# One fused attention and MLP kernel: where lam multiplies the channel mix, and how the planner orders the engine queues

## The chip, the cores and the metric

The kernel runs on one core of a Trainium2 chip. The metric is the device time of one execution in microseconds (us): 377.52 is the median of 8 runs of the kernel before, from 376.94 to 379.87. TensorE (PE) multiplies matrices into PSUM, which has eight banks; VectorE (DVE), ScalarE (ACT) and GpSimd (POOL) work on elements; SyncE (SP) issues nearly all DMA transfers. Every engine works through its own queue in order.

## What is computed

Batch 8, 8 heads of 64, sequence 576, model width 512. Inputs and output are float32.

```
kv  = einsum('bhsd,bhde', k, v)          # linear attention, no softmax
o   = einsum('bhsd,bhde', q, kv)
x   = o / sqrt(mean(o*o over the head) + 1e-6) * g_norm      # heads side by side: (b, s, 512)
a1  = alpha1 * x + beta1
u   = x + lam * (w_tok @ a1)             # token mix, 576 x 576
a2  = alpha2 * u + beta2
out = u + lam * (max(a2 @ w_ch1, 0) @ w_ch2)                 # channel mix, 512 -> 2048 -> 512
```

## The kernel before

The program is not written in the order in which it runs. `Prog.op` records each operation with a cost for each engine that could do it, the tiles that it reads and writes, and a priority. `Prog.schedule` is a list scheduler that plays the whole program through with these costs. It picks the engine, the PSUM bank and the place in the queue of each operation, and `emit` writes the queues out in that order. On the chip each queue is then fixed: an instruction whose input is late holds up all that stand behind it on its engine. A load is believed to land at `dma_free + 2.0`, where `dma_free` starts at 1.2 us and grows by the operation's `dma_us`: 2.8 for a megabyte, 1.4 for half of one, 0.9 for a tail of 64 rows.

A batch goes through these steps, and the scheduler interleaves them over neighbouring batches:

- `load` and `round_in`: q, k and v come in blocks of 1 MB into six staging buffers `st` and are cast to float32r (L521, L414, L415); rows 512 to 575 come apart as tails (L529). Casts go to ScalarE or VectorE, whichever the planner finds free.
- `kv` (L594) and `qtr` (L583, with `identr`): 128x128 float32r matmuls. They are kind "F", which the planner likes to alternate with the bf16 matmuls of another step.
- `norm`: o by L583, its square on ScalarE (L651), the sum over a head (L653), root (L656), reciprocal (L659) and the product (L664) on VectorE and ScalarE. From it come `rt`, the input of the token mix, on VectorE (L666), and x itself on GpSimd (L669).
- `tok` (L887): five matmuls for each of five row chunks; VectorE adds the result to x (L895), and a cast gives `ub`.
- `ut` (L915): transposes of `ub`, evicted as `a2t` with alpha2 and beta2 (L924, L926).
- `ch1` (L957): 64 matmuls of 512 columns for an even batch, 128 of 320 for an odd one, which takes the tail rows of two batches along. Relu into `ht` on ScalarE or VectorE (L942, L943).
- `ch2` (L977): 16 matmuls for each row chunk, four chunks for an even batch and five for an odd one. VectorE adds the result to x in place (L985), and SP stores x. For batch 0 the order runs over blocks of w_ch2 and then chunks, so its four chunks end close together. lam is already in the weights: `load_w2` multiplies each block of w_ch2 by `lam_bc` as it casts it to bf16, one half on VectorE and one on GpSimd (L1166).

Batch 0 has a path of its own in `first`, in two halves of four heads each. Its squares' sums are made by matmuls with a wide selector `sel` onto 4 rows (L781), the root is taken there (L788), five small transposes bring it into columns (L792), and VectorE takes the reciprocal (L795). The token weights are cast with row sums (L1109, L1110), transposed (L1134) and copied from PSUM. While nothing of `ch1` has begun, `dummy` puts matmuls on ones (L1060) where PE would be idle, in any PSUM bank if three are free. Weights come in this order after batch 0: w_tok, four blocks of w_ch1 (cast by ScalarE, L414), batch 1, four blocks of w_ch2.

Of the kernel before, what the change touches and what calls it, by code (L numbers as in the profile page):

```python
# [7 lines left out]
F32 = mybir.dt.float32  # L8
# [6 lines left out]
NB = 8  # L15
# [8 lines left out]
class Op:  # L24
    __slots__ = ("cost", "fn", "deps", "raw", "alloc", "tiles", "pri", "idx", "eng", "kind",
                 "start", "end", "pos", "waits", "inc", "lat", "clock", "sem", "succ", "left",
                 "ready", "keep", "soft", "tag")

    def __init__(self, cost, fn, pri, idx):
        self.cost, self.fn, self.pri, self.idx = cost, fn, pri, idx  # L30
        self.deps, self.raw = set(), set()
        self.alloc, self.tiles = [], []
        self.start = self.end = self.pos = self.eng = None
        self.waits, self.inc, self.lat, self.clock, self.sem = [], False, None, None, None
        self.succ, self.left, self.ready, self.kind, self.keep, self.soft = [], 0, 0.0, None, 0, set()

# [13 lines left out]
class Prog:  # L50
# [20 lines left out]
    def op(self, engs, fn, r=(), w=(), pri=0.0, dma_us=None, kind=None, keep=0, after=()):  # L71

        o = Op(dict(engs), fn, pri, len(self.ops))
        o.lat, o.kind, o.keep, o.tag = dma_us, kind, keep, self.tag
        self.ops.append(o)
# [44 lines left out]
    def schedule(self):  # L120
# [11 lines left out]
        dma_free = 1.2  # L132
# [4 lines left out]
        last_kind = None  # L137
        seq = []
# [27 lines left out]
        def bank_ok(b):  # L166
            tile = owner[b]
            return tile is None or all(x.end is not None and x.end <= t + 1e-9 for x in tile.ops)
# [28 lines left out]
        def finish(e, o):  # L197
            return max(free[e], t) + o.cost[e]

        def choose(e):  # L200
            q = ready[e]
            back, pick, second = [], None, None
            while q:
# [12 lines left out]
                if not fits(o):  # L216
                    continue
# [16 lines left out]
        while left:  # L234
            progressed = True
            while progressed:
                progressed = False
                for e in engines:
# [19 lines left out]
                    free[e] = t + cost  # L258
                    if o.lat is not None:
# [21 lines left out]
            if self.warm is not None and free["PE"] <= t + 1e-9 and t > 0.5:  # L281
                o = self.dummy(t, owner, bank_ok, since)
# [22 lines left out]
    def dummy(self, t, owner, bank_ok, since):  # L305
        okb = [b for b in range(8) if bank_ok(b)]
        if len(okb) < 3:
            return None
        b = min(okb, key=since)
        tile = PTile(self, 1)  # L310
        tile.bank = b
        o = Op({"PE": 0.22}, lambda e, n, tile=tile: self.warm_fn(e, tile), 0, 10 ** 6 + len(self.ops))
        self.ops.append(o)
        o.idx = len(self.ops) + 10 ** 6
# [3 lines left out]
        if any(y.end is None or y.end > t for y in self.warm_deps):  # L318
            self.ops.pop()
            return None  # L320
        if owner[b] is not None:
            o.deps.update(owner[b].ops)
        tile.ops.append(o)
        owner[b] = tile
# [83 lines left out]
def pool_us(n, two=True):  # L408
    return 0.2 + n * (2.5 if two else 1.05) / 1000.0
# [8 lines left out]
def bass_transnormer_attn__then__resmlp_affine_kernel(  # L418
# [15 lines left out]
    with ExitStack() as stack:  # L434
# [9 lines left out]
        vcol = sb("vcol", [8, 128], F32)  # L444
        cols = sb("cols", [128, 8], F32)
        ones = sb("ones", [1, 128], F32)
# [4 lines left out]
        sel = sb("sel", [128, 2, 128], F32R)  # L451
# [17 lines left out]
        yn = sb("yn", [128, 3, DM], F32)  # L469
        xm = sb("xm", [128, 2, 4, DM], F32)  # L470
# [17 lines left out]
        rs4 = w2f[0:4, 0:2 * TP].rearrange("p (x s) -> p x s", x=2)  # L488
        e1 = w2f[:, 1280:1792]
        sel0 = w2f[:, 1792:2048].rearrange("p (i c) -> p i c", i=2)  # L490
# [24 lines left out]
        def load_main(n, src, b, eng, pri, halves=None):  # L515
# [3 lines left out]
            for x in halves or (None,):  # L519
# [4 lines left out]
                    w=STK(i) if x is None else [("st", i, x)], dma_us=2.8 if x is None else 1.4,  # L524
                    pri=pri, kind="L")

        def load_tail(n, tile, src, b, lo, eng, pri):
# [3 lines left out]
                w=[key], dma_us=0.9, pri=pri, kind="L")  # L531

        def load(b, pri):
            P.tag = "load.%d" % b
            if b == 0:
# [5 lines left out]
                load_tail("q", qft, q, b, 0, "SP", pri)  # L541
                load_main("k", k, b, "SP", pri, (1,))
                load_main("v", v, b, "SP", pri, (1,))
                load_main("q", q, b, "SP", pri, (1,))
# [11 lines left out]
        def round_in(b, pri):  # L556
            P.tag = "round_in.%d" % b
            for n, dst in (("q", qr), ("k", kr), ("v", vr)):
                i = held[n, b]
                pieces = [(c, c + 2, 0, 8) for c in (0, 2)]  # L560
                for c0, c1, h0, h1 in pieces:
                    def f(e, m, i=i, c0=c0, c1=c1, h0=h0, h1=h1, n=n, d=dst):
# [7 lines left out]
                         w=[(n + "r", x, y) for x in range(c0, c1) for y in hs], pri=pri)  # L570
            for n, lo, dst in (("k", 0, krt), ("v", 64, vrt)):
                P.op({"DVE": 0.45, "ACT": 0.65}, lambda e, m, lo=lo, d=dst: copy_to(
                    e, m, flat(d[0:64]), flat(kvft[lo:lo + 64])), r=[n + "ft"], w=[n + "rt"], pri=pri)
            if b % 2 == 0 or b == 1:
                rows = {0: slice(0, 64), 1: slice(64, 128)}.get(b, slice(0, 128))
                P.op({"DVE": 0.45, "ACT": 0.65}, lambda e, m: copy_to(
                    e, m, flat(qrt[rows]), flat(qft[rows])), r=["qft0", "qft1"][:b + 1], w=["qrt"], pri=pri)
# [8 lines left out]
        def kv(b, pri):  # L586
            P.tag = "kv.%d" % b
            t = P.ptile(1)
            for pr in range(4):
                for c in range(5):  # L590
                    def f(e, _, pr=pr, c=c):
                        a = flat(kr[:, c, 2 * pr:2 * pr + 2, :] if c < 4 else krt[:, 2 * pr:2 * pr + 2, :])
                        m = vr[:, 2 * pr:2 * pr + 2, c, :] if c < 4 else vrt[:, 2 * pr:2 * pr + 2, :]
                        return e.matmul(t.flat()[:, 128 * pr:128 * pr + 128], a, m,  # L594
                                        start=(c == 0), stop=(c == 4))
                    P.op(F, f, r=["krt", "vrt"] if c == 4 else [("kr", c, pr // 2), ("vr", c, pr // 2)],
                         w=[t], pri=pri, kind="F", keep=2, after=[("kvc", b % 2, x) for x in range(4)])
            for h in range(2):
                rows = slice(64 * h, 64 * h + 64)
                P.op({"ACT": act_us(256), "DVE": dve_us(256)}, lambda e, m, h=h, rows=rows: copy_to(  # L600
                    e, m, kvc[rows, b % 2, :, 64 * h:64 * h + 64],
                    t.flat(rows).rearrange("p (r x) -> p r x", r=4)[:, :, 64 * h:64 * h + 64]),
                    r=[t], w=[("kvc", b % 2, pr) for pr in range(4)], pri=pri - 5)
# [32 lines left out]
        def norm(b, pri):  # L636
            P.tag = "norm.%d" % b
            def chunk(c):
# [6 lines left out]
                for pr in range(4):  # L645
# [22 lines left out]
                    r=[("yn", s3), "ge1"], w=[rkey(b, c)], pri=p - 2)  # L668
# [7 lines left out]
        def first(pri):  # L676
# [6 lines left out]
            def rounding(x):  # L683
                P.tag = "round.0%d" % x
                for n, dst in (("k", kr), ("v", vr), ("q", qr)):
                    i = held[n, 0]
                    hs = slice(4 * x, 4 * x + 4)
                    for c in (0, 2):
                        def f(e, m, i=i, c=c, n=n, d=dst):
# [5 lines left out]
                             r=[("st", i, x)], w=[(n + "r", y, x) for y in (c, c + 1)], pri=pri)  # L695

            P.tag = "round.t"
            for n, lo, dst in (("k", 0, krt), ("v", 64, vrt)):
                P.op({"DVE": 0.45, "ACT": 0.65}, lambda e, m, lo=lo, d=dst: copy_to(
                    e, m, flat(d[0:64]), flat(kvft[lo:lo + 64])), r=[n + "ft"], w=[n + "rt"], pri=pri)  # L700
            P.op({"DVE": 0.45, "ACT": 0.65}, lambda e, m: copy_to(
                e, m, flat(qrt[0:64]), flat(qft[0:64])), r=["qft0"], w=["qrt"], pri=pri)

            def attend(x):
# [13 lines left out]
                for h in range(2):  # L718
                    rows = slice(64 * h, 64 * h + 64)
                    P.op({"ACT": act_us(128), "DVE": dve_us(128)}, lambda e, m, h=h, rows=rows, t=t: copy_to(  # L720
                        e, m, kvc[rows, 0, 2 * x:2 * x + 2, 64 * h:64 * h + 64],
                        t.flat(rows).rearrange("p (r y) -> p r y", r=2)[:, :, 64 * h:64 * h + 64]),
                        r=[t], w=KVK, pri=pri)
# [4 lines left out]
                    r=["g"] + KVK, w=[("kr", 0, x)], pri=pri + 3)  # L728
# [38 lines left out]
                for i in range(2):  # L767
# [4 lines left out]
                        kind="T", keep=1)  # L772
                P.op({"ACT": act_us(128)}, lambda e, _, t=t: e.activation(
# [3 lines left out]
                ts, tt = P.ptile(1), P.ptile(1)  # L777
                for t, n in ((ts, 512), (tt, 64)):
                    for i in range(2):
                        pr = 2 * x + i  # L780
                        P.op({"PE": 0.216 if n == 512 else 0.117}, lambda e, _, t=t, n=n, i=i, pr=pr: e.matmul(  # L781
                            t.flat()[:, 0:n], sel[:, i, :],
                            sqt[:, pr, :] if n == 512 else sqtt[:, pr, 0:64],
                            start=(i == 0), stop=(i == 1)),
                            r=["sel", (("vr", 0, x) if i == 0 else ("vr2", x)) if n == 512 else ("kr", 1, x)],
                            w=[t, ("sums", x)], pri=pri + 3, kind="T")
                for t, lo, n in ((ts, 0, 512), (tt, 512, 64)):
                    P.op({"ACT": act_us(n)}, lambda e, _, t=t, lo=lo, n=n: e.activation(  # L788
                        rs4[:, x, lo:lo + n], t.flat(slice(0, 4))[:, 0:n], ACT.Sqrt, bias=eps[0:4, :],
                        scale=1.0 / DH), r=["eps", t, ("rs4", 2)], w=[("rs4", x, lo)], pri=pri)  # L790
                for c in range(5):
                    P.op({"PE": 0.1}, lambda e, _, c=c: e.transpose(  # L792
                        tt.flat()[:, 128 + 4 * c:132 + 4 * c], rs4[:, x, 128 * c:128 * c + 128],
# [464 lines left out]
```

## Time and profile before

| What | Measured |
|---|---|
| median of 8 runs | 377.52 us |
| the profiled execution | 378.22 us |
| its span, first to last instruction | 376.4 us |
| PE busy | 362.8 us, 96% of the span |
| DVE busy | 225.9 us, 60% |
| ACT busy | 176.7 us, 47% |
| POOL busy | 86.6 us, 23% |
| granted TensorE clock, mean over the span | 0.993 |
| read from HBM, written | 38.20 MB, 9.44 MB |
| PE matmul groups L957, L977, L887 | 146.8, 140.1, 50.6 us |

In the profile, times count from the first instruction. A row names the engine, the source line of the kernel, the operation, and what is written from what; `x8` after it is a count of instructions. In brackets stands how long the engine was idle before it, and what let it go on. "PEld" is the weight load that belongs to a matmul and overlaps the matmul before it. Matmul ends are modelled, so neighbouring matmuls overlap in the rows, and their pace is read from start to start.

### The profile page before, as it was taken

What the parts mean: (1) busy time and instruction counts of PE and PEld (TensorE: products, weight loads), DVE (VectorE), ACT (ScalarE), POOL (GpSimd) and SP (SyncE); (2) the same over time, 40 slices, a digit from 0 to 9 for tenths busy, and PEclk for the clock granted to TensorE, in tenths of its full rate; (3) what the DMA queues carried; (4) which work ended last, traced back from release to release, by engine and by line L of the source; (5) the groups of instructions that cost most, each with busy time, mean ns of one, the idle gap of its engine ahead of it and who ended that gap; (6) DMA issues with size and microseconds to landing.
All of it is one profiled execution on the core that took longest, in us unless ns stands there. A gap on an engine that the chain in (4) does not pass through costs nothing.

```text
span 376.4 us, 5601 instructions
## 1 busy us (share of the span) xinstructions
PE 362.8 (96%) x2258; PEld 224.4 (60%) x2258; DVE 225.9 (60%) x390; ACT 176.7 (47%) x310; POOL 86.6 (23%) x73
## 2 busy tenths in 40 slices
PE   8998699999999999999999999999999999999994
PEld 2786465569775564556865565557755544557641
DVE  5578569995985688539936595539534682520011
ACT  2689646666864256125741266134731274116400
POOL 4641087610441133003500123003500340000000
PEclk9999989999999999999999999999999999999999
DMA  6999999999959228311000120011000210020021
GB/s 197 312 340 361 274 383 310 286 279 319 306 141 311 91 58 290 73 57 56 2 2 22 62 57 0 2 56 57 0 2 28 84 29 1 30 84 2 0 84 56
DMA packets 47797, 47.99 MB, mean 128 GB/s; under 512 B 14096, under 2 KB 38680, under 8 KB 47772
## 3 DMA queue, kind: packets, MB, share of 16 engines
q1 hardware_dynamic: 47520, 47.47, 42.3%
q8 instruction: 17, 0.28, 0.3%
q10 hardware_dynamic: 252, 0.18, 0.2%
q14 instruction: 8, 0.07, 0.1%
HBM read 38.20 MB, written 9.44 MB: 127 GB/s over the span
## 4 chain that ended last, share of the span: by engine, by line
PE 76%; DMA 9%; DVE 6%; SPq 4%; ACT 2%; issue 1%; DVEq 0%; ACTq 0%
PE ps L977 32%; PE ps L957 27%; PE ps L887 10%; DMA st<-in_moe_w_ch_dram 4%; DMA st<-in_v_dram 3%; PE ps L583 3%; DMA kvft<-in_v_dram 2%; PE ps L915 2%; PE ps L594 2%; SPq L521 2%; SPq L529 2%; DVE w L1166 1%; ACT w L414 1%; DVE ht L943 1%; DVE small L653 1%; SPq L1017 1%
## 5 line engine op out<-in xcount | busy, mean ns | idle before, releaser
L957 PE MATMUL ps<-a2t,w 128*128 128x320 bf16 (+1 forms) x768 | 146.8, 332 | 2.1 <-ACT kvc L414 0.7
L977 PE MATMUL ps<-w,ht 128*128 128x512 bf16 x576 | 140.1, 381 | 0.1
L957 PEld LDWEIGHTS ps<-a2t,w 128*128 128x128 bf16 x768 | 73.4, 98 | 44.7 <-DVE ht L943 1.5
L942 ACT ACTIVATE ht<-ps 128x640 bf16<-128x640 f32 (+1 forms) x105 | 68.0, 649 | 47.1 <-PE ps L957 46.7
L977 PEld LDWEIGHTS ps<-w,ht 128*128 128x128 bf16 x576 | 54.5, 98 | 59.1 <-DVE yn L664 0.6
L669 POOL TENSOR_TENSOR xm<-yn,g_bc 128x512 f32<-128x512 f32 x28 | 46.0, 1642 | 167.7 <-DVE yn L664 167.2
L985 DVE TENSOR_TENSOR xm<-ps,xm 128x512 f32<-128x512 f32 x32 | 21.9, 688 | 55.5 <-PE ps L977 55.0
L651 ACT ACTIVATE sq<-ps 128x512 f32<-128x512 f32 (+1 forms) x35 | 20.6, 590 | 49.0 <-PE ps L583 48.9
L895 DVE TENSOR_TENSOR xm<-ps,xm 128x512 f32<-128x512 f32 x28 | 19.3, 690 | 38.0 <-PE ps L887 36.8
L887 PE MATMUL ps<-rt,wt 128*128 128x512 bf16 x140 | 37.3, 381 | 0.0
L594 PE MATMUL ps<-vr,kr 128*128 128x128 f32 x112 | 34.6, 394 | 2.6 <-DVE ht L943 2.6
L583 PE MATMUL ps<-kvc,qt 128*128 128x128 f32 x112 | 33.2, 386 | 0.5 <-DVE ht L943 0.5
L583 PE MATMUL ps<-identr,qr 128*128 128x128 f32 x112 | 31.2, 374 | 0.9 <-ACT qr L414 0.9
L924 ACT ACTIVATE a2t<-ps,cols 128x640 bf16<-128x640 bf16 (+1 forms) x15 | 11.7, 829 | 41.1 <-PE ps L915 41.1
L653 DVE TENSOR_REDUCE small<-sq 128x8 f32<-128x512 f32 (+1 forms) x35 | 23.6, 675 | 10.3 <-ACT sq L651 10.0
L594 PEld LDWEIGHTS ps<-vr,kr 128*128 128x128 f32 x112 | 23.2, 207 | 3.4 <-DVE ht L943 3.1
L664 DVE TENSOR_TENSOR yn<-ps,small 128x512 f32<-128x512 f32 (+1 forms) x35 | 24.0, 685 | 0.5
L666 DVE TENSOR_TENSOR rt<-yn,ge 128x512 bf16<-128x512 f32 x28 | 24.0, 856 | 0.5
L583 PEld LDWEIGHTS ps<-kvc,qt 128*128 128x128 f32 x112 | 22.3, 200 | 3.0 <-DVE ht L943 0.8
L583 PEld LDWEIGHTS ps<-identr,qr 128*128 128x128 f32 x112 | 22.0, 200 | 1.5 <-DVE a2t L926 1.0
L887 PEld LDWEIGHTS ps<-rt,wt 128*128 128x128 bf16 x140 | 13.5, 98 | 15.2
L414 ACT ACTIVATE qt<-ps 128x512 fp32r<-128x512 f32 (+1 forms) x29 | 15.7, 556 | 7.0 <-PE ps L583 6.7
(145 smaller groups left out, 376.4 us busy)
## 6 DMA issues: line engine op xcount, KB each, us to landing
st<-in_moe_w_ch_dram SPq DMA_DIRECT2D x8, 1024.0 KB, 12.5
out_dram<-xm SPq DMA_DIRECT2D x32, 256.0 KB, 2.3
st<-in_q_dram SPq DMA_DIRECT2D x7, 1024.0 KB, 7.9
st<-in_k_dram SPq DMA_DIRECT2D x7, 1024.0 KB, 10.5
st<-in_v_dram SPq DMA_DIRECT2D x7, 1024.0 KB, 12.3
ht<-in_moe_w_tok_dram SPq DMA_DIRECT2D x2, 576.0 KB, 9.5
kvft<-in_k_dram SPq DMA_DIRECT2D x8, 128.0 KB, 9.2
kvft<-in_v_dram SPq DMA_DIRECT2D x8, 128.0 KB, 7.7
```

The source lines that it names most:

```text
L583: P.op(F, lambda e, _: e.matmul(t.flat()[:, 128 * pr:128 * pr + 128], a(), m(), start=True, stop=True), r=r, w=[t], kind="F", **kw)
L594: return e.matmul(t.flat()[:, 128 * pr:128 * pr + 128], a, m, start=(c == 0), stop=(c == 4))
L651: P.op({"ACT": act_us(512)}, lambda e, _: e.activation(flat(sq[rows, s2]), t.flat(rows), ACT.Square), r=[t], w=[("sq", s2)], pri=p)
L653: P.op({"DVE": dve_us(512)}, lambda e, _: e.tensor_reduce(out=small[rows, s4], in_=sq[rows, s2], axis=AX.X, op=ALU.add), r=[("sq", s2)], w ...
L664: P.op({"DVE": dve_us(512)}, lambda e, _: e.tensor_tensor(out=hview(yn[rows, s3, :]), in0=hview(t.flat(rows)), in1=bc, op=ALU.mult), r=[t, ...
L666: P.op({"DVE": dve_us(512), "POOL": pool_us(512)}, lambda e, _: e.tensor_tensor(out=rto, in0=yn[rows, s3, :], in1=ge1[rows, :], op=ALU.mul ...
L669: P.op({"POOL": pool_us(512)}, lambda e, _: e.tensor_tensor(out=hview(x), in0=hview(yn[rows, s3, :]), in1=g_bc[rows, None, :].to_broadcast ...
L887: return e.matmul(t.flat(), wt[:, sc, col:col + 128], rt[:, sc, :] if sc < 4 else rtt[:], start=(sc == 0), stop=(sc == 4))
L942: return e.activation(dst, src(), ACT.Relu)
L957: return e.matmul(o, w1[:, dj, 128 * fj:128 * fj + 128], m, start=(dj == 0), stop=(dj == 3))
L977: P.op({"PE": 0.216}, lambda e, _: e.matmul(t.flat(), ht[:, fj, 128 * c:128 * c + 128], w2[:, fj, :], start=(fj == 0), stop=(fj == 15)), r ...
L985: P.op({"DVE": dve_us(512)}, lambda e, _: e.tensor_tensor(out=x, in0=t.flat(), in1=x, op=ALU.add), r=[t] + keys, w=keys, pri=p - 2)
```

## The change

Six things change together.

1. lam leaves the weights. `load_w2` only casts, on ScalarE, VectorE or GpSimd. In `ch2` VectorE multiplies the PSUM result by `lam_bc` into a new SBUF tile `lc` (one buffer), and GpSimd adds `lc` to x in place; in the last batch VectorE may do the add.
2. [...] Loads start at 3.4 us and take 3.0 a megabyte, 1.5 a half, 1.0 a tail.
3. The warming matmuls have bank 7 for themselves until `ch1` begins.
4. In `first`, the squares' sums come as ten matmuls straight into columns, so the five transposes go; the two halves of `kvc` are evicted without a wait for each other; the second half of q is loaded ahead of those of k and v; one more product of `rt` goes to GpSimd; the token weights are transposed once all five casts are done, and their copies alternate between ScalarE and VectorE; `ut(0)` puts two groups into one PSUM bank and evicts all four on VectorE.
5. `kv(1)` streams each operand twice (256 columns, two PSUM tiles) and is no longer kind "F".
6. Priorities at the start change; casts of w_ch1 wait, in the plan only, for the last root of batch 0, and those of the fourth block may go to GpSimd in place of VectorE.

```diff
-        dma_free = 1.2
+        dma_free = 3.4
+        ports = [0.0]
+        def shares(e, o):
+            return o.lat is None and (e == "POOL" or e == "DVE" and o.port)
...
         def bank_ok(b):
+            if b == 7 and self.warm is not None:
+                return False
...
         def finish(e, o):
-            return max(free[e], t) + o.cost[e]
+            at = max(free[e], t)
+            if shares(e, o):
+                at = max(at, ports[0])
+            return at + o.cost[e]
...
+                if shares(e, o) and ports[0] > t + 1e-9:
+                    continue
...
+                    if shares(e, o):
+                        ports[0] = t + cost
...
 def pool_us(n, two=True):
-    return 0.2 + n * (2.5 if two else 1.05) / 1000.0
+    return 0.2 + n * (2.2 if two else 0.9) / 1000.0
...
+        lc = sb("lc", [128, DM], F32)
...
                 load_main("q", q, b, "SP", pri, (0,))
                 load_tail("q", qft, q, b, 0, "SP", pri)
+                load_main("q", q, b, "SP", pri, (1,))
                 load_main("k", k, b, "SP", pri, (1,))
                 load_main("v", v, b, "SP", pri, (1,))
-                load_main("q", q, b, "SP", pri, (1,))
...
         def kv(b, pri):
-            t = P.ptile(1)
+            wide = b == 1
+            tiles = [P.ptile(1) for _ in range(2 if wide else 1)]
...
+                        if wide:
+                            o = tiles[pr // 2].flat()[:, 256 * (pr % 2):256 * (pr % 2) + 256]
+                            m = m[:, None].to_broadcast([128, 2, 2, DH])
...
-                ts, tt = P.ptile(1), P.ptile(1)
-                for t, n in ((ts, 512), (tt, 64)):
+                ts = P.ptile(1)
+                for c in range(5):
                     for i in range(2):
                         pr = 2 * x + i
-                        P.op({"PE": 0.216 if n == 512 else 0.117}, lambda e, _, t=t, n=n, i=i, pr=pr: e.matmul(
-                            t.flat()[:, 0:n], sel[:, i, :],
-                            sqt[:, pr, :] if n == 512 else sqtt[:, pr, 0:64],
+                        P.op({"PE": 0.12}, lambda e, _, c=c, i=i, pr=pr: e.matmul(
+                            ts.flat()[:, 4 * c:4 * c + 4],
+                            sqt[:, pr, 128 * c:128 * c + 128] if c < 4 else sqtt[:, pr, :],
+                            sel[:, i, :], start=(i == 0), stop=(i == 1)),
...
+                P.root = P.op({"ACT": 0.25}, lambda e, _, ro=ro: e.activation(
+                    ro, ts.flat()[:, 0:20], ACT.Sqrt, bias=eps[:], scale=1.0 / DH),
+                    r=["eps", ts], w=[("rs", x)], pri=pri)
+                P.op({"DVE": 0.25}, lambda e, _, ro=ro: e.reciprocal(ro, ro), r=[("rs", x)],
+                     w=[("rs", x)], pri=pri)
...
-                    P.op({"POOL": pool_us(256 * n)} if x == 0 else {"DVE": dve_us(256 * n)},
+                    P.op({"POOL": pool_us(256 * n)} if x == 0 or c0 == 0 else {"DVE": dve_us(256 * n)},
...
+                    o = P.op({"ACT": act_us(n, 2), "DVE": 0.53 if n == 512 else dve_us(n)} if b else
+                             {"DVE": 0.53}, g, r=[t, "cols"], w=[("a2t", dj)], pri=pri - 5)
+            for djs in ((0, 1), (2, 3)) if b == 0 else ((0,), (1,), (2,), (3,)):
+                group(djs)
...
-                P.op({"DVE": dve_us(512)}, lambda e, _: e.tensor_tensor(
-                    out=x, in0=t.flat(), in1=x, op=ALU.add), r=[t] + keys, w=keys, pri=p - 2)
+                o = P.op({"DVE": dve_us(512)}, lambda e, _: e.tensor_tensor(
+                    out=lc[:], in0=t.flat(), in1=lam_bc[:], op=ALU.mult), r=[t, "lam"],
+                    w=["lc"], pri=p - 2)
+                o.raw.update(o.deps)
+                P.op({"POOL": pool_us(512)} if b < NB - 1 else {"POOL": pool_us(512), "DVE": dve_us(512)},
+                     lambda e, _: e.tensor_tensor(out=x, in0=x, in1=lc[:], op=ALU.add),
+                     r=["lc"] + keys, w=keys, pri=p - 2, port=True)
...
-                P.op({"ACT": act_us(512)} if qn < 3 else {"ACT": act_us(512), "DVE": dve_us(512, 2)}, f, r=STK(i),
-                     w=[("w1", qn, j)], pri=pri)
+                P.op({"ACT": act_us(512)} if qn < 3 else {"ACT": act_us(512), "POOL": pool_us(512, False)}, f,
+                     r=STK(i), w=[("w1", qn, j)], pri=pri).soft.add(P.root)
...
-                P.op({"POOL": pool_us(1024)} if hh else {"DVE": dve_us(1024)}, lambda e, _, hh=hh: e.tensor_tensor(
-                    out=w2[:, 4 * n + 2 * hh:4 * n + 2 * hh + 2, :],
-                    in0=st[:, i, 1024 * hh:1024 * hh + 1024].rearrange("p (j c) -> p j c", j=2),
-                    in1=lam_bc[:, None, :].to_broadcast([128, 2, DM]), op=ALU.mult),
-                    r=STK(i) + ["lam"], w=[("w2", n, hh)], pri=pri + 70)
+                P.op({"ACT": act_us(1024), "DVE": dve_us(1024, 2), "POOL": pool_us(1024, False)},
+                     lambda e, m, hh=hh: copy_to(
+                    e, m, w2[:, 4 * n + 2 * hh:4 * n + 2 * hh + 2, :].rearrange("p j c -> p (j c)"),
+                    st[:, i, 1024 * hh:1024 * hh + 1024]),
+                    r=STK(i), w=[("w2", n, hh)], pri=pri + 70, port=True)
...
-            if o.pri < -500 and o.tag == "sums.01":
-                o.pri -= 2
+            if o.pri < -500 and o.tag == "wt":
+                o.pri -= 4
+            if o.pri < -500 and o.tag in ("kv.01", "qtr.01", "sums.01"):
+                o.pri -= 6
             if o.pri < -500 and o.tag[:2] == "w1":
-                o.pri += 30
+                o.pri = -480 + 4 * int(o.tag[3])
```

## Prediction

> **What bounds the kernel now.** I read the page's busy rows and slices first, then a table of stretches, then the order of time around the one bad stretch. The slices (40 of 9.4 us each; tenths busy, tenths of the clock, tenths of the DMA engines):
>
> ```profile
> PE   8998699999999999999999999999999999999994
> DVE  5578569995985688539936595539534682520011
> PEclk9999989999999999999999999999999999999999
> DMA  6999999999959228311000120011000210020021
> ```
>
> TensorE is the bound from slice 6 to the end; the only hole is slice 5 (38 to 47 us), and the only dip of the clock follows in slice 6. Until slice 10 the DMA engines are full. So a change that touches VectorE, ScalarE or GpSimd is worth something in three places only: the front (until the first channel product runs without a break, at 38 us), the hole, and the tail after the last matmul. The stretches (us; busy of PE, PEld, DVE, ACT, POOL; clock; DMA):
>
> ```profile
> 26.90:38.00 11.10, 9.61 (x82) 7.21 (x81) 9.99 (x26) 10.19 (x19) 1.72 (x4) 1.00 1.07 364
> ...
> 43.00:46.00 3.00, 0.44 (x2) 0.19 (x1) 2.31 (x4) 1.85 (x3) 0.00 (x0) 1.00 1.10 261
> 46.00:51.00 5.00, 4.65 (x23) 3.08 (x22) 2.93 (x4) 2.47 (x5) 2.30 (x1) 0.66 1.05 387
> 51.00:60.00 9.00, 8.46 (x58) 5.77 (x56) 7.38 (x6) 4.83 (x9) 8.76 (x4) 1.00 1.07 366
> 60.00:83.60 23.60, 23.54 (x148) 13.75 (x146) 22.54 (x38) 15.94 (x26) 10.54 (x7) 1.00 1.11 280
> ```
>
> From 43 to 46 PE does 0.44 us: 2.56 lost. From 46 to 51 it is idle for 0.35, and a mean clock of 0.66 is 1.7 us lost. The hole costs 4.6 us; 51 to 60 loses 0.54 more. The timeline tells why:
>
> ```profile
> 43.30 0.69 DVE L415 CAST vr<-st 128x1024 fp32r<-128x1024 f32 x1 [2.75 <-DMA st<-in_v_dram]
> ...
> 44.36 1.27 DVE L943 TENSOR_SCALAR ht<-ps 128x512 bf16<-128x512 f32 x2
> ...
> 45.69 0.19 PEld L594 LDWEIGHTS ps<-vr,kr 128*128 128x128 f32 x1 [3.05 <-DVE ht L943]
> ```
>
> VectorE stands 2.75 us at the cast of v of batch 1, whose load has not landed. Two relus (L943) are queued behind it, their PSUM banks stay taken, and PE, also in order, waits for them with 64 x 0.216 = 13.8 us of ch1(0) not finished. It was not short of work: the queues were in the wrong order. The planner believed the load earlier. Its own constants put v(1) at 1.2 + 11.1 (batch 0: 3 x 0.9 + 6 x 1.4) + 3.6 (w_tok) + 11.2 (w_ch1) + 8.4 (q, k, v) + 2.0 = 37.5 us; the trace has 43.30.
>
> **The change, part by part.** The profiled run took 378.22 us, 1.82 around a span of 376.4, 0.70 above the median of 377.52. I count differences, so they hold for the median as well.
>
> *Load constants (3.4 at the start, 3.0 a MB, 1.5 a half, 1.0 a tail).* v(1) is now believed at 3.4 + 12.0 + 3.6 + 12.0 + 9.0 + 2.0 = 42.0, 1.3 before the trace; the first w_ch2 block at 48.0 (before 43.0), where the trace has a VectorE cast of it released at 48.66. So relus and ch1(0) should stand ahead of the v cast. At most 4.6 us come back; at least none, if another load takes this place. [...] I take 3.8.
>
> *The front.* For heads 4 to 7 the trace has the squares' sums from 23.94 (L781), two roots on 4 rows, five transposes, and the reciprocal ending at 27.27: 3.3 us. The new form is ten matmuls onto 4 columns (f32 weight loads of 0.19 us that overlap at about 0.11, as L807's do: 1.1), a root of 0.3 (L656's row), a reciprocal of 0.28 and three handoffs of 0.1 to 0.2: 2.1. That is 1.2 off. The two halves of kvc no longer wait for each other (DVE at 19.12, ACT at 20.50): up to 1.1 off. The token weights have two of five PSUM copies fewer on VectorE, and all transposes in one go; before, the last copy ended at 27.58 and tok.00 began at 27.85, so this path must shorten as well or nothing moves. Moving q's second half ahead of k and v brings k and v about 1.5 us later (16.1 to 17.6), which eats part. After 27 us the stretch is filled by VectorE (9.99 of 11.1) and ScalarE (10.19); there the change gives one 0.68 multiply to GpSimd and takes one a2t (0.53): no gain, it only starts earlier. ScalarE loses some casts of w_ch1 to GpSimd (1.0 each there). Ends: 3.3 off to 1 on; I take 1.8 off, nearer the sum's row.
>
> *The cast of w_ch2.* Out go eight multiplies by lam, in come eight plain copies on any of three engines:
>
> ```profile
> 48.70 12.42 POOL L1166 TENSOR_TENSOR w<-st,lam_bc 128x1024 bf16<-128x1024 f32 x4 [15.91 <-DMA st<-in_moe_w_ch_dram]
> ...
> 51.36 1.82 DVE L1166 TENSOR_TENSOR w<-st,lam_bc 128x1024 bf16<-128x1024 f32 x1 [1.48 <-DMA st<-in_moe_w_ch_dram]
> ...
> 55.74 3.17 DVE L1166 TENSOR_TENSOR w<-st,lam_bc 128x1024 bf16<-128x1024 f32 x1
> ```
>
> VectorE's four took 8.4 us against 1.22 for the one that began before GpSimd's; a copy of that size takes 0.69 (the v cast above), 1.05 on ScalarE. With four on VectorE it has 8.4 - 2.8 = 5.6 us more room between 48 and 62. PE only idles 0.54 there: 0.5 off, between 0 and 0.8.
>
> *kv(1) twice as wide.* Its 20 matmuls hid between bf16 ones (a pair is issued every 0.29 us, a bf16 one alone every 0.216: 0.074). As 256 columns, eight like them (L737) take 1.12 us, 0.14 each. 20 x 0.066 = 1.3 on; a narrow one that has no partner takes 0.25, so at the other end the wide form saves 2.
>
> *The channel add.* The multiply into lc reads PSUM and lam_bc and has the form of today's add, 0.69: nothing more on VectorE. The add goes to GpSimd for batches 0 to 6, 31 of them:
>
> ```profile
> L669 POOL TENSOR_TENSOR xm<-yn,g_bc 128x512 f32<-128x512 f32 x28 | 46.0, 1642 | 167.7 <-DVE yn L664 167.2
> L985 DVE TENSOR_TENSOR xm<-ps,xm 128x512 f32<-128x512 f32 x32 | 21.9, 688 | 55.5 <-PE ps L977 55.0
> ...
> L666 DVE TENSOR_TENSOR rtt<-yn,ge 64x512 bf16<-64x512 f32 x7 | 10.1, 1436 | 0.1
> ```
>
> 1.28 (an L669 that ran alone) to 1.64 each: 40 to 51 us on an engine busy for 86.6 of 376. [...] lc is a single buffer: the next multiply waits for the add, and behind it on VectorE everything. Chunks lie 3.45 us apart (2.76 idle + 0.69 in L985's rows), and 0.69 + 1.28 fits. Only batch 0's four chunks end close together, 4 x 0.216 = 0.86 apart: up to 3 x 1.2 = 3.6 us of VectorE. SP's stores go out 1.4 later, and so do the loads queued behind them, some 20 us before their use. I take 0.2 on, up to 4.
>
> *The tail.* In batch 7 the planner may choose VectorE (0.69 against 1.33), and does. Today the end hangs on this:
>
> ```profile
> 370.95 0.69 DVE L985 TENSOR_TENSOR xtl<-ps,xtl 128x512 f32<-128x512 f32 x1 [2.76 <-PE ps L977]
> ```
>
> A second such instruction follows it before the store: 0.69 + 0.06 = 0.75 on, certain.
>
> *Bank 7 for the warming matmuls* leaves seven banks in the front; PE had clock 1.00 there and the bank waits were 0.4 or less: 0, within 0.5 either way.
>
> Sum: -3.8 - 1.8 - 0.5 + 1.3 + 0.2 + 0.75 = -3.85. **377.5 - 3.85 = 373.7 us.**
>
> **Rivals.** *The hole only moves.* DMA is full until 115 us, so an earlier front waits longer for the same data. For it: w_ch2 lands where it did. Against it: the 13.8 us of ch1(0) plus the attention of batch 1 cover 38 to 53. Then 377.5 - 1.8 - 0.5 + 2.25 = 377.5, no change.
>
> *VectorE sets the start of ch1(1): slower.* From 46 to 83.6 VectorE does 2.93 + 7.38 + 22.54 = 32.85 us and PE had other work until ch1(1) began. By my count it falls to 32.85 - 8.4 + 2.8 + 1.2 + 1.3 = 29.7, and PE wants to be there 5.6 us sooner, in 32. [...] It decides once VectorE's work there is over 0.95 x 37.6 = 35.7.
>
> **How the numbers follow.** Forecast 0.60, all faster. The moved hole 0.20: 0.06 faster, 0.10 same, 0.04 slower. VectorE 0.20, slower. A difference under 0.3%, 1.1 us, can't be told from none. Faster 0.66, same 0.10, slower 0.24. Low end: the hole gone (4.6), the front 3.3, casts 0.8, against a tail of 0.75 and nothing for kv(1), and 1 of the small losses near 95 us: 368.5. High end: into the VectorE case, 381.0. The likeliest case alone: 369 to 376.
>
> **What would show it.** Right: slice 5 of PE at 9 and no dip of the clock; L594 never waiting 2 us for a relu; the stretch from 46 to ch1(1) with less VectorE time; one more VectorE row of 0.69 after the last matmul. Wrong: a PE wait at L957 or L977 for a2t or rt of batch 1 between 60 and 85, with VectorE full of waits behind GpSimd; or the first unbroken L957 no earlier than 38.

## The result, and the profile after

The changed kernel takes **373.93 us** (median of 11 runs, 371.99 to 374.65), the kernel before 377.96 beside it (32 runs): a ratio of 0.9888, 95% interval 0.987 to 0.9906. That is 4.0 us less; the forecast was 3.85 less. The profiled execution took 371.63 us, 2.3 below the median of its runs, with a span of 369.5, so differences between profiles come out a little larger than those between medians.

The slices of the changed kernel (each 9.2 us; tenths, as before):

```profile
PE   8999999999999999999999999999999999999993
...
DVE  4788679974985896648853781638452794410132
...
PEclk9999999999999999999999999999999999999998
DMA  7999999999467129020000110011001110020021
```

The hole in slice 5 is gone, the dip of the clock in slice 6 is gone, and the DMA engines have spare time from slice 11 on, where before they were still at 9 (the prediction has them full only until slice 10). The stretches (columns as before; the bounds follow the work, which starts earlier):

```profile
43.00:46.00 3.00, 3.00 (x26) 2.89 (x25) 1.80 (x4) 1.85 (x3) 0.00 (x0) 1.00 1.01 366
46.00:51.00 5.00, 5.00 (x36) 3.43 (x35) 3.17 (x7) 3.15 (x6) 1.04 (x1) 1.00 1.05 400
51.00:60.00 9.00, 9.00 (x49) 4.49 (x47) 8.18 (x15) 6.20 (x12) 3.52 (x3) 1.00 1.11 364
60.00:77.50 17.50, 17.13 (x117) 11.14 (x115) 16.85 (x25) 11.03 (x17) 7.29 (x6) 1.00 1.03 345
```

From 43 to 60 PE loses nothing, where before it lost 5.15 us, clock included. The last column is what the DMA engines moved: 400 GB/s from 46 to 51 (387 before), 366 from 43 to 46 (261 before). The timeline of VectorE has the reason why the hole closed:

```profile
39.43 0.69 DVE L423 CAST vr<-st 128x1024 fp32r<-128x1024 f32 x1 [0.83 <-DMA st<-in_v_dram]
...
363.38 0.69 DVE L1016 TENSOR_TENSOR lc<-ps,lam_bc 128x512 f32<-128x512 f32 x1 [2.04 <-PE ps L1008]
364.10 0.69 DVE L1021 TENSOR_TENSOR xtl<-xtl,lc 128x512 f32<-128x512 f32 x1
```

The queue of VectorE changed only a little here: two relus and a cast of qt stand ahead of the cast of v(1), where before it was one relu, and two relus still stand behind it. What changed more is the load: the cast begins 3.9 us earlier (39.43 against 43.30), and VectorE waits 0.83 us for it and not 2.75. The last two rows are the longer tail, a multiply and then an add.

### The profile page after: what moved, and what is told of

Its sections match the earlier page's. It is cut to its first block, busy times and chain, and to the rows that moved or that the text cites. A ratio compares the mean times of both kernels' runs of the same rounds, so it can differ in the third digit from the quotient of the medians.

```text
span 369.5 us, 5712 instructions
## 1 busy us (share of the span) xinstructions
PE 361.0 (98%) x2279; PEld 224.2 (61%) x2279; DVE 223.7 (61%) x393; ACT 176.3 (48%) x304; POOL 119.5 (32%) x113
## 3 DMA queue, kind: packets, MB, share of 16 engines
q1 hardware_dynamic: 47520, 47.47, 38.1%
## 4 chain that ended last, share of the span: by engine, by line
PE 94%; DVE 3%; ACT 1%; issue 0%
PE ps L988 35%; PE ps L1008 31%; PE ps L916 10%; PE ps L591 5%; PE ps L1095 3%; PE ps L609 3%; PE ps L946 2%; PE ps L865 1%; DVE rt L692 1%; DVE yn L690 1%; PE ps L836 1%; PE ps L741 1%; PE ps L1108 1%; PE ps L768 1%; DVE small L679 0%; PE ps L1169 0%
## 5 line engine op out<-in xcount | busy, mean ns | idle before, releaser
L988 PE MATMUL ps<-a2t,w 128*128 128x320 bf16 (+1 forms) x768 | 142.2, 329 | 0.8 <-ACT ht L973 0.4
L973 ACT ACTIVATE ht<-ps 128x640 bf16<-128x640 f32 (+1 forms) x103 | 67.1, 653 | 44.6 <-PE ps L988 43.8
L1021 POOL TENSOR_TENSOR xm<-xm,lc 128x512 f32<-128x512 f32 x28 | 37.4, 1334 | 129.5 <-DVE lc L1016 129.5
L1016 DVE TENSOR_TENSOR lc<-ps,lam_bc 128x512 f32<-128x512 f32 x36 | 24.8, 690 | 66.5 <-PE ps L1008 65.8
L695 POOL TENSOR_TENSOR xm<-yn,g_bc 128x512 f32<-128x512 f32 x28 | 43.2, 1543 | 37.8 <-DVE yn L690 36.7
L677 ACT ACTIVATE sq<-ps 128x512 f32<-128x512 f32 (+1 forms) x35 | 20.5, 593 | 47.9 <-PE ps L591 47.7
L924 DVE TENSOR_TENSOR xm<-ps,xm 128x512 f32<-128x512 f32 x28 | 19.2, 689 | 31.0 <-PE ps L916 29.8
L609 PE MATMUL ps<-vr,kr 128*128 128x128 f32 (+1 forms) x112 | 30.9, 370 | 0.0
L692 DVE TENSOR_TENSOR rt<-yn,ge 128x512 bf16<-128x512 f32 x26 | 25.1, 971 | 0.5
L954 ACT ACTIVATE a2t<-ps,cols 128x640 bf16<-128x640 bf16 (+1 forms) x11 | 8.9, 841 | 32.8 <-PE ps L946 32.8
L609 PEld LDWEIGHTS ps<-vr,kr 128*128 128x128 f32 x112 | 21.7, 200 | 0.3
```

Source lines behind the costliest of these rows:

```text
L609: return e.matmul(o, a, m, start=(c == 0), stop=(c == 4))
L692: P.op({"DVE": dve_us(512), "POOL": pool_us(512)}, lambda e, _: e.tensor_tensor(out=rto, in0=yn[rows, s3, :], in1=ge1[rows, :], op=ALU.mul ...
L695: P.op({"POOL": pool_us(512)}, lambda e, _: e.tensor_tensor(out=hview(x), in0=hview(yn[rows, s3, :]), in1=g_bc[rows, None, :].to_broadcast ...
L973: return e.activation(dst, src(), ACT.Relu)
L988: return e.matmul(o, w1[:, dj, 128 * fj:128 * fj + 128], m, start=(dj == 0), stop=(dj == 3))
L1016: o = P.op({"DVE": dve_us(512)}, lambda e, _: e.tensor_tensor(out=lc[:], in0=t.flat(), in1=lam_bc[:], op=ALU.mult), r=[t, "lam"], w=["lc"] ...
```

## The experiments

Each kernel was timed in turn with the kernel before on the same chip; three chips were used for experiments 1 to 11 (1 to 4, 5 to 8, 9 to 11), and a further set of runs for experiment 12. Between groups the ratios are compared, inside a group the times too. "Packets of 1 KB" are the transfers of 1024 bytes that start between 1 and 29 us of the span, nearly all of them the 3072 of batch 0 (q, k and v), with their mean duration in the trace: **59.7 ns in the kernel before, 50.6 in the changed one**. A hole is measured from the start of the last matmul before it to the start of the next.

### One part of the change at a time

**1. Load constants alone**, in the kernel before:

```diff
-        dma_free = 1.2
+        dma_free = 3.4
...
-                w=STK(i), dma_us=2.8, pri=pri, kind="L")
+                w=STK(i), dma_us=3.0, pri=pri, kind="L")
```

> The kernel before, with only the planner's load constants of the change (3.4 at the start, 3.0 a MB, 1.5 a half, 1.0 a tail). Theory, the hole is a matter of the believed landing of batch 1's v: 378.0 - 3.8 = 374.2 us, no stretch near 43 us in which PE waits 2 us for a relu, no half clock. Rival A, the room on VectorE from the plain casts of w_ch2 closes it: 378, hole still there. Rival B, the new front and its priorities close it: 378.

Measured: 378.53 us against 377.05, ratio 1.0034 (1.0007 to 1.0061). A hole stays, 2.11 us long at 41.6 (2.94 before), and the timeline of VectorE has it wait at the same cast.

```profile
39.38 1.28 DVE L943 TENSOR_SCALAR ht<-ps 128x512 bf16<-128x512 f32 x2
43.00 0.69 DVE L415 CAST vr<-st 128x1024 fp32r<-128x1024 f32 x1 [2.34 <-DMA st<-in_v_dram]
43.61 0.68 DVE L943 TENSOR_SCALAR ht<-ps 128x512 bf16<-128x512 f32 x1
```

Two relus now stand ahead of the cast and one behind it (third row), where before it was one and two. At this place the constants do help. Two stretches of the kernel before, then of this one (columns as before):

```profile
38.00:60.00 22.00, 18.55 (x111) 12.23 (x109) 14.16 (x17) 11.68 (x20) 11.06 (x4) 0.92 1.10 331
70.00:120.00 50.00, 49.27 (x379) 36.91 (x378) 41.45 (x68) 34.07 (x56) 12.98 (x9) 1.00 0.98 282
...
38.00:60.00 22.00, 20.27 (x130) 13.23 (x131) 14.27 (x21) 14.68 (x27) 11.86 (x4) 1.00 1.09 335
70.00:120.00 50.00, 46.03 (x349) 34.64 (x352) 43.30 (x68) 28.29 (x46) 12.36 (x10) 1.00 1.01 287
```

From 38 to 60 PE is idle for 1.73 us in place of 3.45, and the clock, which cost another 1.7 before, holds: 3.4 us come back. From 70 to 120 PE is idle for 3.97 us in place of 0.73, and most of it is gone again. These are single profiles, and why the new order loses there was not tried. The constants alone do not bring the gain.

**2. The changed kernel with the old load constants.** In this kernel, and in 3 and 4, the product into yn also waits for VectorE's own earlier reads of that buffer.

```diff
-        dma_free = 3.4
+        dma_free = 1.2
...
+                o.raw.update(o.deps)
```

> The changed kernel with the old load constants (1.2, 2.8, 1.4, 0.9). Theory: the hole comes back, 373.9 + 3.8 = 377.7 us. Rivals A and B: 374, within 1 us of the changed kernel, since casts and front are as in the change.

Measured: 372.49 against 377.05, ratio 0.9873 (0.9841 to 0.9905); no hole, packets of 1 KB at 51.6 ns. So without the step that was to bring 3.8 us the whole gain is there.

**3. Only lam moved**, in the kernel before (multiply into lc, add on GpSimd, plain casts of w_ch2). To make room for lc, sel is cut to 32 columns, and two small tiles of the front (ones and vcol) go into w2's space, as in the change.

```diff
-        sel = sb("sel", [128, 2, 128], F32R)
+        sel = sb("sel", [128, 2, 32], F32R)
...
+                o = P.op({"DVE": dve_us(512)}, lambda e, _: e.tensor_tensor(
+                    out=lc[:], in0=t.flat(), in1=lam_bc[:], op=ALU.mult), r=[t, "lam"],
```

> The kernel before, with only lam moved: plain casts of w_ch2 on any of three engines, lc on VectorE, the add on GpSimd (VectorE may do it in the last batch). Theory: casts 0.5 off, lc 0.2 and tail 0.75 on, so 378.0 + 0.4 = 378.4 us and the hole stays. Rival A: 374. Rival C, that the add on GpSimd stops VectorE in the start: 380 or more.

Measured: 379.28 against 377.05, ratio 1.0051 (1.0029 to 1.0072). The hole stays, 3.35 us long at 42.4; packets of 1 KB take 60.2 ns.

**4. The changed kernel with lam back in the weights:**

```diff
-                o = P.op({"DVE": dve_us(512)}, lambda e, _: e.tensor_tensor(
-                    out=lc[:], in0=t.flat(), in1=lam_bc[:], op=ALU.mult), r=[t, "lam"],
...
+                P.op({"POOL": pool_us(1024)} if hh else {"DVE": dve_us(1024)}, lambda e, _, hh=hh: e.tensor_tensor(
```

> The changed kernel with lam back in the weights: w_ch2 multiplied by lam on VectorE and GpSimd, the sum added in place by VectorE as before. Theory: tail 0.75 and lc 0.2 off, casts 0.5 on: 373.9 - 0.4 = 373.5 us. Rival A: the hole comes back, 377 to 378.

Measured: 373.36 against 377.05, ratio 0.9895 (0.9859 to 0.9931), not to be told from experiment 2. Its timeline shows what the plain casts do away with: beside GpSimd's own casts VectorE's take up to three microseconds, and PE waits a microsecond for one.

```profile
47.34 3.09 DVE L1197 TENSOR_TENSOR w<-st,lam_bc 128x1024 bf16<-128x1024 f32 x1
...
61.16 0.82 PE L1009 MATMUL ps<-w,ht 128*128 128x512 bf16 x3 [1.04 <-DVE w L1197]
```

After these four, the kernels with fast packets (the changed one, 2, 4) gain 1.0% to 1.3%, and those with slow packets (1, 3) gain nothing, whichever part of the plan they have. What the three that gain share is the place of the staging tiles in SBUF. Tiles are laid out in the order in which they are declared. The change takes two tiles of 512 bytes a partition (vcol, ones) from ahead of `st` and shrinks `sel` from 1024 bytes to 32: 2016 bytes, which is eight times 256 less 32. So `st`, `kvft` and `qft`, the targets of all loads of q, k, v, w_ch1 and w_ch2, move from 224 bytes past a multiple of 256 to a multiple of 256. In experiment 3 the sizes move by 1792, seven times 256, and the targets stay at 224. The sizes give the shifts against the kernel before, and it is the shifts that the runs test; the absolute place, 224, stands in no trace.

### The address alone

**5. The kernel before with 32 unused bytes a partition:**

```diff
+        pad0 = sb("pad0", [128, 8], F32)
         st = sb("st", [128, NS, 2048], F32)
```

> The kernel before with one unused SBUF tile of 32 bytes a partition declared ahead of the staging buffers st, and nothing else; every queue keeps its order. It moves st, kvft and qft from 224 to 0 past a multiple of 256 bytes, and xm, xtl and ht from 0 to 32. New theory, the address of the load targets sets the pace of the loads: packets of 1024 bytes in the start fall from 60 to 51 ns, v of batch 1 lands about 3 us earlier, the hole shrinks, 377.1 - 3 = 374 us. Rival, the new front sets the gain and the pace of the loads only follows: 377, packets at 60 ns.

**6. The changed kernel with 224 unused bytes** at the same place (56 columns in place of 8):

> The changed kernel with 224 unused bytes ahead of st, and nothing else: st, kvft, qft go from 0 to 224 past a multiple of 256, xm, xtl, ht from 32 to 0, as in the kernel before. New theory: packets of 1024 bytes go from 51 to 60 ns, loads land 3 us later, and most of the gain is lost: 376 to 377 us. Rival, the front: 373 to 374.

Measured, on one chip, beside 377.67 for the kernel before and 372.56 for the changed kernel with all targets at multiples of 256 (experiment 8):

| | targets at 224 past a multiple of 256 | targets at a multiple of 256 |
|---|---|---|
| plan before | 377.67 us | **372.56**, ratio 0.9868 (0.9847 to 0.9888) |
| plan changed | **375.92**, ratio 0.9961 (0.9944 to 0.9979) | 372.56, ratio 0.9869 (0.9845 to 0.9893) |
| packets of 1 KB | 59.7 and 61.9 ns | 50.2 and 49.6 ns |

32 unused bytes give the kernel before all that the change gave, with the queues as they were. They move every tile that is declared behind them, not the load targets alone; that the loads are what they speed up is read from the packets. The page shows the difference in two places. First the kernel before: what the DMA engines moved in each slice, then the queue (packets, MB, share of the 16 engines over the span).

```profile
GB/s 197 312 340 361 274 383 310 286 279 319 306 141 311 91 58 290 73 57 56 2 2 22 62 57 0 2 56 57 0 2 28 84 29 1 30 84 2 0 84 56
...
q1 hardware_dynamic: 47520, 47.47, 42.3%
```

The same of the kernel before with 32 unused bytes:

```profile
GB/s 203 356 382 385 325 392 281 362 369 321 109 245 211 57 106 294 2 85 30 0 2 28 78 38 0 2 58 57 0 2 57 58 28 1 30 85 2 0 85 57
...
q1 hardware_dynamic: 47520, 47.47, 38.2%
```

And of the changed kernel with 224 unused bytes:

```profile
GB/s 172 314 347 363 247 386 333 257 309 328 324 159 320 72 56 266 101 56 58 0 2 28 58 57 2 0 56 58 2 0 28 86 28 0 31 78 8 0 86 56
...
q1 hardware_dynamic: 47520, 47.47, 41.8%
```

Packets and bytes are the same to the last digit; only the time that they took differs. A packet's mean time is the share times 16 engines times the span: 0.423 x 16 x 376.4 us / 47520 = 53.6 ns before, 0.382 x 16 x 370.6 / 47520 = 47.7 with the 32 bytes. In slices 2 to 4 the loads come at 312 to 361 GB/s in the one and at 356 to 385 in the other. The stretches of the kernel before with 32 unused bytes show the same hole closed, with no change of plan:

```profile
38.00:43.00 5.00, 4.64 (x32) 3.32 (x33) 4.60 (x10) 4.60 (x8) 0.00 (x0) 1.00 1.01 299
43.00:46.00 3.00, 3.00 (x20) 2.03 (x19) 2.59 (x4) 1.76 (x4) 0.92 (x1) 1.00 0.99 373
46.00:51.00 5.00, 5.00 (x36) 3.49 (x34) 3.16 (x4) 2.96 (x6) 4.92 (x2) 1.00 1.04 398
51.00:60.00 9.00, 8.95 (x55) 5.56 (x56) 8.84 (x12) 6.43 (x12) 8.70 (x4) 1.00 1.11 371
```

From 43 to 60 PE loses 0.05 us at full clock, against 5.15 before; the medians differ by 5.11. The cast of v(1) begins 2.6 us earlier than before (43.30), and VectorE doesn't wait for it at all:

```profile
40.67 0.68 DVE L415 CAST vr<-st 128x1024 fp32r<-128x1024 f32 x1
```

**8. Other tiles that move.** In the changed kernel `xm`, `xtl` and `ht` stand 32 bytes past a multiple of 256, where before they were on one. 224 more bytes ahead of `xm` put them back.

```diff
+        pad1 = sb("pad1", [128, 56], F32)
         xm = sb("xm", [128, 2, 4, DM], F32)
```

> The changed kernel with 224 unused bytes ahead of xm: st, kvft, qft stay at a multiple of 256, and xm, xtl, ht come to one too. If the address counts on the reading side of the stores as well, stores get faster, but they are hidden: within 0.5 us of the changed kernel, at best 0.5 less by w_tok landing earlier in ht.

Measured: 372.56 us, ratio 0.9869 (0.9845 to 0.9893), which overlaps the changed kernel's own 0.9888. The stores' side is worth nothing that was measured; `st`, `kvft` and `qft` are what counts. `ht` is a load target too, of w_tok: its packets of 4608 bytes took 178 ns (median) both here and in the changed kernel.

**9 and 10. Other offsets**, in the kernel before: 96 and 160 unused bytes put the load targets 64 and 128 past a multiple of 256.

> The kernel before with one unused tile of 96 bytes a partition ahead of st, so that the load targets st, kvft and qft start 64 bytes past a multiple of 256 (224 in the kernel before, 0 in the run with 32 unused bytes). [...] If only a multiple of 64 bytes counts, packets take 50 to 51 ns and the time is that of the aligned run, 372.6. If any start off a multiple of 256 costs the same, packets take 59 to 60 ns, the hole of 2 to 3 us is there and the time is 377 to 378.

> The same with 160 unused bytes, so that the load targets start 128 bytes past a multiple of 256. If the cost grows with the offset: packets of 1 KB take 54 to 57 ns and the time is 373.5 to 376.5 us, between the run at 64 and the kernel before. If only a multiple of 64 counts: 50 to 51 ns and 372.6. If any start off a multiple of 256 costs the same: 59 to 60 ns and 377 to 378.

| Offset of the targets | Packets of 1 KB | Time | Ratio |
|---|---|---|---|
| 0 (experiment 5) | 50.2 ns | 372.56 us | 0.9868 (0.9847 to 0.9888) |
| 64 | 60.2 | 377.29 | 0.9976 (0.996 to 0.9992) |
| 128 | 58.3 | 375.13 | 0.993 (0.9913 to 0.9947) |
| 224 (the kernel before) | 59.7 | 377.92 | 1 |

That a multiple of 64 is enough is ruled out, and so is a cost that grows with the offset: 64 is as dear as 224. The nearest of the three expectations is that any start off a multiple of 256 costs about the same. What it doesn't give is the 2.2 us between 64 and 128. The profiles differ in the clock. At 64:

```profile
PEclk9999989999999999999999999999999999999999
```

At 128:

```profile
PEclk9999999999999999999999999999999999999999
```

At 64 PE waits 2.46 us and the clock falls in slice 6, at 128 it waits 2.10 and the clock holds. From 46 to 51 us the clock is 0.67 at 64 and 1.00 at 128: 0.33 x 5 = 1.65 us, most of the difference; but v(1) was also cast 2.0 us earlier at 128 (42.09 against 44.06) with packets only 3% shorter, and why is open. The 14 runs at 64 go from 375.55 to 378.17, the six at 128 from 374.76 to 375.73, so the profile of 64, at 378.17, is the slowest of its runs.

### The rest of the change

**7. kv(1) narrow**, in the changed kernel:

```diff
-            wide = b == 1
+            wide = False
```

> The changed kernel with kv(1) as before: 20 matmuls of 128 columns that may pair with bf16 ones. The prediction's step: 1.3 us less, 372.6. Against it: the wide form was free because nothing waited for PE there, or the narrow ones find no partner: 373 to 374 or more.

Measured: 372.95 us, ratio 0.9882 (0.9859 to 0.9905), beside 372.56 for the wide form in experiment 8. No cost of the wide form can be seen.

**12. Do the constants order the queues, when loads are slow?** Experiment 6 had slow loads and no hole. This one is experiment 2 with 224 unused bytes: slow loads, the changed plan, the old constants.

> The changed kernel with 224 unused bytes ahead of st, so that loads are as slow as before, and with the old load constants besides (and the wait of VectorE on its own product yn, as in the run with the old constants alone). The run with 224 bytes and the new constants took 375.92 us against 377.4 before and had no hole in ch1(0), although v(1) was cast at 44.09. If the new constants are what put the relus ahead of that cast, as the prediction has it, then the hole of 2 to 3 us comes back here and the time is 377.5 to 380 us. If they don't decide it, PE has no idle time over 1 us between 38 and 52, and the time is that of the run with the new constants, 375.5 to 376.5.

Measured: 375.97 against 376.86, ratio 0.9975 (0.9955 to 0.9996). With the new constants (experiment 6), VectorE's timeline has two relus ahead of the cast of v(1):

```profile
40.83 1.29 DVE L975 TENSOR_SCALAR ht<-ps 128x512 bf16<-128x512 f32 x2
...
44.09 0.69 DVE L423 CAST vr<-st 128x1024 fp32r<-128x1024 f32 x1 [1.06 <-DMA st<-in_v_dram]
```

With the old ones VectorE comes to it early, and PE stops, in the timelines of both engines:

```profile
43.06 0.69 DVE L423 CAST vr<-st 128x1024 fp32r<-128x1024 f32 x1 [2.15 <-DMA st<-in_v_dram]
...
45.14 0.33 PE L592 MATMUL ps<-identr,qr 128*128 128x128 f32 x1 [1.14 <-ACT ht L975]
```

So the constants do what the prediction said of them in the changed kernel too: a gap of 1.5 us at 43.6 goes. But the kernel is not measurably faster by it: ch1(1) begins at 82.03 with the new constants and at 82.33 with the old, and the intervals of the two ratios overlap. The expected hole was longer (2 to 3 us) and the expected time higher (377.5 to 380) than what came.

**11. The last batch done the old way at its end.** All targets aligned as in 8; lam is multiplied into w2 in place while ch1(7) runs, and the last ch2 leaves PSUM by one add.

```diff
+                if b == NB - 1:
+                    P.op({"DVE": dve_us(512)}, lambda e, _: e.tensor_tensor(
+                        out=x, in0=t.flat(), in1=x, op=ALU.add), r=[t] + keys, w=keys, pri=p - 2)
...
+            if b == NB - 1:
+                P.tag = "scale"
```

> The changed kernel with all load targets at multiples of 256 bytes, and the last batch alone done the old way at its end: w2 is multiplied by lam in place on VectorE while TensorE works on ch1(7), and the last ch2 leaves PSUM by one add in place instead of lc and then the add. If the tail of the changed kernel is worth its 0.72 us and the multiplications are hidden, 0.5 to 0.9 us below the same kernel without this step (372.56 against 377.5 there), a ratio near 0.985. If the multiplications delay VectorE's evictions of ch1(7), no gain or a loss of up to 1 us.

Measured: 372.33 against 377.92, ratio 0.985 (0.9829 to 0.9871), the lowest of all. VectorE's timeline ends in one row after the last matmul:

```profile
365.64 0.69 DVE L1018 TENSOR_TENSOR xtl<-ps,xtl 128x512 f32<-128x512 f32 x1 [2.76 <-PE ps L1009]
```

The ratio lies 0.0019 below that of experiment 8, 0.7 us, as expected; the intervals overlap, so the size of it is not shown.

## Why the prediction came true, and where its reasons did not

**The total was right, and its largest step was wrong.** The step that failed is the one headed "load constants", -3.8 us: that the new belief of the planner puts the relus ahead of the cast of v(1) and so closes the hole. At the place that it names it is nearly right: alone, the constants give back 3.4 us between 38 and 60 in the profile. What failed is the term in the sum, which let that gain last to the end: 3.2 us of it are lost again between 70 and 120, and the kernel takes 0.34% longer (experiment 1). No run shows the 3.8 itself, which was the author's estimate out of a hole read at 4.6. Without the constants the changed kernel has no hole and all its gain (2); with slow loads they close a gap of 1.5 us, and no gain at the end can be measured (6 and 12). In their place stands something that the prediction did not have among its steps or rivals: the loads became faster, because their targets came to lie on multiples of 256 bytes. That alone, with the old queues, gives 5.1 us (5). So it is luck that the total came out: 3.85 was summed from terms that the runs do not bear out, and what was measured is the gain of an address.

The place and the price of the loss were read rightly. The prediction put the hole at 4.6 us, with 0.54 after it, and the kernel whose only edit is 32 bytes takes back 5.1. What was taken as fixed was the landing of v(1) at 43.30: the prediction asked who waits for it, not why it came so late. One thing to ask about was there: in the whole diff (the lines are not in the excerpt above) `vcol` and `ones` go and `sel` shrinks, which moves everything declared behind them. No line of the trace before shows what that is worth.

**The rest of the change, by itself, is worth less than forecast.** At the old address it gains 0.39% (0.21% to 0.56%), 1.75 us between the medians, where the sum had 3.85, and at the new one nothing that can be measured (372.56 against 372.56). There the profiles have the last matmul begin 1.5 us earlier with the changed plan (363.22 against 364.70), and the tail takes half of that back. So "the hole only moves", given 0.20, describes the change without its address better than the forecast did: in experiment 6 PE is idle for only 0.25 us between 38 and 60, but the unbroken run of ch1(0) begins at 39.49, 1.4 us later than before.

*The front*, -1.8: in the profile after, the unbroken run of ch1(0) begins 3.07 us earlier (35.00 against 38.07), but with faster loads; at the old address it begins later, as said. The clock blurs both readings: its record begins, at full speed, at 13.03 us in the profile before and at 4.27 in the profile after, and has a half clock from 9.1 to 15.9 in that of experiment 6. No run took the front apart, so its share is open.

*Bank 7*, 0: no run took it apart. The clock of 1.00 that the prediction read for the front is recorded only from 13.03 us on.

*The casts of w_ch2*, -0.5: four went to ScalarE at 1.05 us, three to VectorE at 0.69, one to GpSimd at 1.04; with lam in the weights PE waits 1.04 us for them (4). The direction holds, the time does not tell it.

*kv(1)*, +1.3: mis-sized. The wide matmuls take 0.28 us and cost nothing in the whole (7).

*The channel add*, +0.2: as read. The page of the changed kernel has the two groups:

```profile
L1021 POOL TENSOR_TENSOR xm<-xm,lc 128x512 f32<-128x512 f32 x28 | 37.4, 1334 | 129.5 <-DVE lc L1016 129.5
L1016 DVE TENSOR_TENSOR lc<-ps,lam_bc 128x512 f32<-128x512 f32 x36 | 24.8, 690 | 66.5 <-PE ps L1008 65.8
```

An add takes 1334 ns, inside the 1.28 to 1.64 of the prediction, the multiply beside it keeps its 690, and the longest wait of the multiply for lc was 0.19 us. The 0.2 was the author's estimate, and no run shows it by itself. That lam moved alone costs 0.51% (3) is not all a price of the add: its hole was longer too, 3.35 us against 2.94, and the clock fell for 6.8 us and not 3.4 (0.84 from 43 to 46, 0.50 from 46 to 51, 0.95 from 51 to 60).

*The tail*, +0.75: the second row begins 0.72 after the first; right.

*Rival "VectorE sets the start of ch1(1)"*: from 46 to 77.5 VectorE did 3.17 + 8.18 + 16.85 = 28.2 us, below the 29.7 counted and far from the 35.7 from which it decides. It was 96% busy from 60 to 77.5, yet PE lost 0.37 us there. No run shows the VectorE case at which the range was given its high end, 381.0: the highest median of all was 379.28 (3), with the hole still in it.

*The clock* fell after holes of 2.94 us (before: 0.66 from 46 to 51) and 2.46 us (9: 0.67 there), and held at 1.00 after 2.11 (1) and 2.10 (10). Where the limit lies the profiles do not show: in that of experiment 5 the clock fell at 8.98 us, 3.4 us after it had risen, with no gap between matmul starts over 1.44 us in between.

## What to carry to other kernels

When tiles are added, removed or resized, look at where the ones declared behind them now stand, the targets of DMA loads above all: here packets of 1 KB took 58.3 to 61.9 ns with the targets 64, 128 or 224 bytes past a multiple of 256, and 49.3 to 51.6 on one. An unused tile of a few bytes is a cheap test of this before any plan is changed; here one of 32 bytes was worth 5.1 us. When a run keeps its hole but loses time, look at the later stretches as well: a gain at one place can be given back at another. When a wait for a load ends the critical stretch, ask first why the load is late (the mean time of its packets, at the same packets and bytes) and only then what should stand ahead of the wait. A change whose total comes out as forecast still needs its largest step undone alone: here that run, and the one with only 32 bytes, turned the explanation round.

## What the runs showed of the hardware

In this kernel the loads of q, k, v, w_ch1 and w_ch2 were slower with their targets 64, 128 or 224 bytes past a multiple of 256 than on one. Packets of 1 KB took 58.3 to 61.9 ns at these three offsets in seven kernels, and 49.3 to 51.6 at 0 in seven others; over all 24576 of them in an execution it is 52.5 to 54.3 against 48.1 to 48.7, a smaller difference. Against the 50.2 of experiment 5 that is 16% to 23% more in the first 29 us; over the whole execution it is 8% to 13% more. In the same stretch packets of 2 KB took 94.9 to 96.9 against 88.7 to 91.4; the last 1024 packets of 256 bytes, which start after 139 us, took 26.2 to 31.3 against 18.0 to 18.4. The cost did not grow with the offset: 60.2 ns at 64, 58.3 at 128, 59.7 at 224. Other offsets were not run, and why a load takes longer off a multiple of 256 no run shows: only the place of the targets was varied.
